# A mixture-of-experts kernel on one core: the last expert does its second half first, and second-half units are written in pairs

## The chip, the cores and the metric

The kernel runs on one core of a Trainium2 chip. The metric is the device time of one execution in microseconds, the median of three runs. Engines are named as in the profile: PE is TensorE (PEld its weight loads), DVE is VectorE, ACT is ScalarE, POOL is GpSimd, and SPq is the queue from which SyncE issues DMAs.

## The reference, cut to what matters

Three stages follow one another: a linear attention with decaying state over 4 x 8 heads, an MLP with squared ReLU (384 to 2048 to 384) over 3072 tokens, and a mixture of 8 experts, of which each token uses the two with the highest noisy logits. The change touches the last stage alone:

```python
out = np.zeros((N, D), dtype=np.float32)          # 3072 x 384
for e in range(E):                                 # 8 experts
    for k in range(2):
        mask = top2[:, k] == e
        h = np.maximum(x[mask] @ w1[e], 0.0)       # 384 -> 1024
        out[mask] += top2_w[mask, k, None] * (h @ w2[e])   # 1024 -> 384
```

## The kernel before, in words

Every product of two float32 matrices is made from three matmuls: each operand is split into a high part and a low part (ScalarE rounds the high part, VectorE or GpSimd subtracts), and high x high, high x low and low x high are summed in PSUM.

Routing writes the rows of the tokens into a table in DRAM (`sent`), sorted by expert. An expert's places in the table are seven blocks of up to 128 tokens, handled as two units (line 111): unit 0 has blocks 0 to 3, 512 tokens; unit 1 has blocks 4 to 6, of which the last counts 52, 308 tokens in all. Tokens beyond these places are left to `overflow` (line 851), which runs only where there are any. The units are worked off in the `order` of line 1024: (0,0), (1,0), (0,1), (1,1), and then each expert's unit 0 and unit 1.

One unit goes like this.

- `fetch` (line 742) issues the DMAs that bring the unit's token rows, from SP; `turn` (line 758), called for each of three slices of the model dimension, transposes a slice on VectorE into the one buffer `xt`, rounds it to `xh` on ScalarE and makes `xl` on VectorE. Both happen ahead, during an earlier unit.
- `up` (line 774) is one of eight first-layer steps f: nine matmuls (three slices d, three products each) into a PSUM bank, with the weights stationary and the tokens moving, then a relu on ScalarE (`hh`) and its low part on VectorE (`hl`). The banks rotate: steps 0, 1, 3, 4, 6, 7 take two banks in turn, steps 2 and 5 a third one.
- The second layer of a unit 0, and of the last expert's unit 1, is `down` (line 797): one call per block, 24 matmuls with the tokens stationary and 384 columns of weights moving; then `scatter` (line 812) scales the block on ScalarE and adds it to the output by an indirect DMA from GpSimd.
- The second layer of the other unit 1s is `down_t` (line 826), "turned": one call for each third d of the model dimension, 24 matmuls with the weights stationary and the 308 tokens moving, then an eviction to `yT`, on VectorE for d = 1 and on ScalarE for the others. `back` (line 842) transposes each block back in three TensorE transposes, during a later unit, and scatters it.

What the other engines do on the side of a unit comes from two lists. `fill` is handed out over the steps by their costs: turn-backs of an earlier unit, a fetch, four weight splits (`conv_next`, line 1014: ScalarE `hi`, VectorE `lo`, then the DMA for weights three pieces ahead, which reuses the freed buffer), and, in a unit 0, the turns of the same expert's unit 1. `late` is put at fixed places: `put(8.8, fn)` means after second-layer call 0 (steps 0 to 7 are first-layer ones), and the fraction of a place under 8 says after which d of that step. `TURN` (line 85) holds the places of the next unit 0's three slices: after step 7, and twice after second-layer call 0. `TURN_11` (line 84) does the same for expert 0's unit 1, with three slices and four weight splits:

```python
TURN_11 = (7.3, 7.8, 8.81, 8.82, 8.83, 9.8, 9.81)
TURN = (7.8, 8.8, 8.81)
```

The order of the instructions on each engine is the order in which the source issues them (`tc.manual_schedule()`, line 116). The main loop over units is at lines 1025 to 1089. The functions that the diff touches:

Of the kernel before, what the change touches and what calls it, by code (L numbers as in the profile page):

```python
# [8 lines left out]
F32 = mybir.dt.float32  # L9
# [8 lines left out]
P = 128  # L18
# [66 lines left out]
TURN = (7.8, 8.8, 8.81)  # L85
# [3 lines left out]
def body(ctx, tc, r, k, v, w, u, w_in, w_out, w_gate, w_noise, noise, w1, w2, out):  # L89
    nc = tc.nc  # L90
# [3 lines left out]
    E, _, F2 = w1.shape  # L94
    NT = B * S
    KD = DM // P
    NF = FF // P
    NF2 = F2 // P
# [12 lines left out]
    UNITS = ((0, 4), (4, 7))  # L111
# [53 lines left out]
    def bank(tag="att", bufs=3):  # L165
        return ps.tile([P, 512], F32, name=tag, tag=tag, bufs=bufs)
# [7 lines left out]
    L, turned = {}, {}  # L174
# [513 lines left out]
    W, RW, X, GT, HT, YT, IDX = {}, {}, {}, {}, {}, {}, {}  # L688
    pools = {}
# [11 lines left out]
    NW = 4  # L701
# [26 lines left out]
    def tokens(un):  # L728
        a0, a1 = UNITS[un]
        return sum(width(a) for a in range(a0, a1))  # L730

    def width(a):
        return SOME if a == LAST - 1 else P
# [37 lines left out]
            idx = IDX[e, un] = pl.tile([P, UNITS[un][1] - UNITS[un][0]], I32, name=f"id{un}", bufs=2)  # L771
            nc.vector.tensor_copy(idx, GT[e, un][:, 1, :])

    def up(e, un, f, between=None):
        n = tokens(un)
        if f % 3 == 2:
            ph = pools["y"].tile([P, 512], F32, name="ph2")[:, :n]
        else:
            ph = bank("ph", 2)[:, :n]
        qi, fo = divmod(f, NF2 // NW)  # L780
        wh, wl = W[e, qi]
        xh, xl = X[e, un]
        sl = slice(fo * P, (fo + 1) * P)
        m = 0
        for d in range(KD):
            for wt, xt in ((wh, xh), (wh, xl), (wl, xh)):
                nc.tensor.matmul(ph, wt[:, d, sl], xt[:, d, :n], start=(m == 0), stop=(m == 3 * KD - 1))  # L787
                m += 1
            if between:
                between(d)  # L790
        hh = pools["f2"].tile([P, BLK], F32R, name=f"hh{f}")
        hl = pools["f2"].tile([P, BLK], F32R, name=f"hl{f}")
        nc.scalar.activation(hh[:, :n], ph, AF.Relu)  # L793
        nc.vector.scalar_tensor_tensor(hl[:, :n], ph, 0.0, hh[:, :n].bitcast(F32), op0=OP.max, op1=OP.subtract)  # L794
        HT[f] = hh, hl

    def down(e, un, a):
        a0, a1 = UNITS[un]
        w_ = width(a)
        sl = slice((a - a0) * P, (a - a0) * P + w_)  # L800
        py = pools["y"].tile([P, 512], F32, name="y", bufs=2)[:w_, :DM]
        m = 0
        for f in range(NF2):
            qi, fo = divmod(f, NF2 // NW)
            wh, wl = W[e, NW + qi]
            hh, hl = HT[f]
            for ht, wt in ((hh, wh), (hl, wh), (hh, wl)):
                nc.tensor.matmul(py, ht[:, sl], wt[:, fo, :], start=(m == 0), stop=(m == 3 * NF2 - 1))  # L808
                m += 1
        scatter(e, a, py)  # L810

    def scatter(e, a, py):
        w_ = width(a)
        yt = pools["f2"].tile([P, DM], F32, name="yt", bufs=3)[:w_]
        un = unit(a)
        col = a - UNITS[un][0]
        nc.scalar.activation(yt, py, AF.Copy, scale=GT[e, un][:w_, 0, col:col + 1])  # L817
        nc.gpsimd.memset(C["gap"], 0.0)
        st = nc.gpsimd.indirect_dma_start(  # L819
            out=out, in_=yt, in_offset=None, compute_op=OP.add,  # L820
            out_offset=bass.IndirectOffsetOnAxis(ap=IDX[e, un][:w_, col:col + 1], axis=0))
        for other in adds[e]:
            tc.declare_no_dep(st.ins, other.ins, reason="a token is sent to an expert once")
        adds[e].append(st)

    def down_t(e, un, d):
        n = tokens(un)
        py = pools["y"].tile([P, 512], F32, name="y", bufs=2)[:, :n]
        m = 0
        for f in range(NF2):  # L830
            qi, fo = divmod(f, NF2 // NW)
            wh, wl = W[e, NW + qi]
            hh, hl = HT[f]
            sl = slice(d * P, (d + 1) * P)
            for wt, ht in ((wh, hh), (wh, hl), (wl, hh)):
                nc.tensor.matmul(py, wt[:, fo, sl], ht[:, :n], start=(m == 0), stop=(m == 3 * NF2 - 1))  # L836
                m += 1
        if d == 0:
            YT[e] = pools["f2"].tile([P, KD, n], F32, name="yT")
        (nc.vector.tensor_copy if d == 1 else nc.scalar.copy)(YT[e][:, d, :], py)  # L840

    def back(e, un, a):
        m = width(a)
        o = (a - UNITS[un][0]) * P
        pb = bank()
        for d in range(KD):
            nc.tensor.transpose(pb[:m, d * P:(d + 1) * P], YT[e][:, d, o:o + m], ident)
        scatter(e, a, pb[:m, :DM])
# [86 lines left out]
    def run(pieces, n):  # L935
        for p in pieces[:n]:
            p()
        del pieces[:n]
# [8 lines left out]
    for j in range(NB):  # L947
        slots = [[] for _ in range(2 * NF)]

        def put(n, fn, *args):  # L950
            k = int(n)
            slots[k].append((n - k, len(slots[k]), lambda: fn(*args)))
# [61 lines left out]
    def conv_next(eng=None):  # L1014
        conv_e(*todo.pop(0), eng)
        if len(todo) >= AHEAD:
            load_e(*todo[AHEAD - 1])

    def prepare(e, un):
        return [lambda c=c: turn(e, un, c) for c in range(KD)]  # L1020


    N0 = NF2 + UNITS[0][1]
    order = [(0, 0), (1, 0), (0, 1), (1, 1)] + [(e, un) for e in range(2, E) for un in range(2)]
    for e, un in order:
        turned = un == 1 and e < E - 1
        n_up = UNITS[un][1] - UNITS[un][0]
        fill, late = [], {}

        def put(p, *fns):  # L1030
            n, d = int(p), int(p % 1 * 4)
            late.setdefault((n, 3 if n >= NF2 else d), []).extend((p, fn) for fn in fns)

        if un == 0 and e > 1:
            fill += [lambda a=a: back(e - 1, 1, a) for a in range(*UNITS[1])]
        if (e, un) == (0, 0):
            plan = [(fn, i) for fn in (r_rest, r_row) for i in range(TPB)] + [(fn,) for fn in (r_soft1, r_soft2, r_soft3, r_top1, r_top2, r_sel, r_table, r_w1, r_rank, r_w2)]
            plan += [(r_send, *divmod(i, 2)) for i in range(2 * TPB)]
            plan = [(n, lambda fn=fn, args=args: fn(NB - 1, *args)) for n, (fn, *args) in zip(ROUTE_LAST, plan)]
            plan += [(n, lambda i=i: conv_next(nc.gpsimd if i < SPLIT_POOL else nc.vector)) for i, n in enumerate(CONV_E)]  # L1040
            plan += list(zip(TURN_10, prepare(1, 0)))
            plan += [(FETCH, lambda: fetch(0, 1)), (TOTALS, totals)]
            carry = [(n - N0, fn) for n, fn in plan if n >= N0]
            for n, fn in plan:
                if n < N0:
                    put(n, fn)
        elif (e, un) == (1, 0):
            for n, fn in carry:
                put(n, fn)
            for n in range(NW):  # L1050
                put(n + 0.8, conv_next)
            put(NW + 0.8, lambda: fetch(2, 0))
            for n, fn in zip(TURN_01, prepare(0, 1)):
                put(n, fn)
            put(TURN_01[-1], lambda: fetch(1, 1))
        elif (e, un) == (0, 1):
            for n, fn in zip(TURN_11, prepare(1, 1) + [conv_next] * NW):
                put(n, fn)
        else:
            if (e, un) == (1, 1):  # L1060
                fill += [lambda a=a: back(0, 1, a) for a in range(*UNITS[1])]
            if e + 1 < E:
                fill += [lambda: fetch(e + 1, un)] + [conv_next] * NW
            elif un == 0:
                fill += [lambda: None] * NW
            if un == 0:
                fill += prepare(e, 1)
            elif e + 1 < E:
                for n, fn in zip(TURN, prepare(e + 1, 0)):
                    put(n, fn)  # L1070
                if (e, un) == (1, 1):
                    put(TURN[-1], lambda: fetch(3, 0))
        cost = [9.0 * n_up] * NF2 + [60.0 if turned else 72.0] * n_up
        left = sum(cost[:NF2] if turned else cost)

        def do(n, d):
            for _, fn in sorted(late.get((n, d), ()), key=lambda x: x[0]):
                fn()

        for n, c in enumerate(cost):  # L1080
            if n < NF2:
                up(e, un, n, lambda d: do(n, d))
            elif turned:
                down_t(e, un, n - NF2)
            else:
                down(e, un, UNITS[un][0] + n - NF2)
            run(fill, round(len(fill) * c / max(left, c) + 0.25))
            left -= c
            do(n, 3)
    f_ctx.close()  # L1090
    ps_ctx.close()
    overflow()
# [27 lines left out]
```

## Time and profile before

| | |
|---|---|
| time, median of 3 runs | 997.45 us (996.15 to 999.99) |
| profiled execution: span from first to last instruction | 993.8 us |
| profiled execution: time of its own beside the span | not listed apart |
| TensorE busy | 959.2 us, 97% of the span |
| TensorE weight loads busy | 828.1 us, 83% |
| VectorE, ScalarE, GpSimd busy | 546.8, 437.6, 349.6 us |
| second expert layer in the chain of waits | PE y L808 14%, PE y L836 6% of the span |

The page gives the busy time of every engine, then the span in 40 slices, the DMA queues, the chain of work that ended last, and the costliest groups of instructions. The expert stage fills the second half of the span. In the timelines a line gives the start, the duration, the engine, the line of the kernel, the operation and its output and inputs; in brackets stand the idle time before it and what released it. A line's duration can be longer than the distance to the next one on its engine, as instructions overlap at their ends.

### The profile page before, as it was taken

Reading aid. Unit: us, or ns where it says so; the run is one execution under the profiler, and the core shown is the slowest. Engines: PE = TensorE matmul, PEld = TensorE weight load, DVE = VectorE, ACT = ScalarE, POOL = GpSimd, SP = SyncE. Lnnn points to the kernel's source line nnn. Section 1 sums busy time; section 2 is a strip of 40 time slices with the busy share of each in tenths; the row PEclk is TensorE's granted clock in tenths of the full one; section 3 lists DMA queues with packets and bytes.
Section 4 is the critical chain, followed back from the end, with each engine's and each line's share of the span. In section 5 each row is a group of like instructions: output and inputs, shape, how many; then the busy total and the mean of one; then the engine's idle time right before and its main releaser. Section 6 shows DMA issues by size and latency. Waiting matters only on the chain.

```text
span 993.8 us, 17485 instructions
## 1 busy us (share of the span) xinstructions
PE 959.2 (97%) x6807; PEld 828.1 (83%) x6807; DVE 546.8 (55%) x985; ACT 437.6 (44%) x795; POOL 349.6 (35%) x407
## 2 busy tenths in 40 slices
PE   7888999998999999999998999999999999999995
PEld 5666788777778878877886989989999998989895
DVE  7999956534845774572343753554445454544320
ACT  4666745333434444443653642543334334444321
POOL 5555462543563454443030352112121212212121
PEclk7999999999999999999999999999999999999998
DMA  7654469939332343231024457565454454554121
GB/s 174 154 151 144 120 157 299 246 90 278 82 108 62 68 119 78 55 78 51 16 97 110 125 139 130 128 134 117 103 108 110 101 124 91 108 110 74 20 32 22
DMA packets 193291, 112.19 MB, mean 113 GB/s; under 512 B 131728, under 2 KB 185776, under 8 KB 193200
## 3 DMA queue, kind: packets, MB, share of 16 engines
q1 hardware_dynamic: 181776, 91.22, 36.4%
q0 software_dynamic: 10624, 19.74, 10.7%
q8 instruction: 55, 0.90, 0.4%
q14 instruction: 36, 0.29, 0.1%
q10 hardware_dynamic: 800, 0.02, 0.0%
HBM read 74.83 MB, written 36.12 MB: 112 GB/s over the span
## 4 chain that ended last, share of the span: by engine, by line
PE 79%; DVE 9%; DMA 4%; SPq 2%; ACT 2%; issue 2%; POOL 1%; POOLq 0%; ACTq 0%; DVEq 0%
PE ph L787 21%; PE ph L492 15%; PE xo L515 15%; PE y L808 14%; PE y L836 6%; PE att L430 3%; PE att L412 2%; DVE t L269 2%; PE att L548 1%; DVE t L268 1%; DVE gl L504 1%; DMA stg<-in_moe_w_in 1%; DVE t L267 1%; DVE t L273 1%; SPq L535 1%
## 5 line engine op out<-in xcount | busy, mean ns | idle before, releaser
L819 POOL DMA_INDIRECT out<-yt,id x56 | 87.1, 1555 | 326.5 <-ACT yt L817 285.0
L504 DVE TENSOR_TENSOR gl<-g,gh 128x512 fp32r<-128x512 f32 x96 | 84.6, 881 | 142.0 <-ACT gh L502 138.3
L794 DVE SCALAR_TENSOR_TENSOR hl<-ph,hh 128x512 fp32r<-128x512 f32 (+1 forms) x128 | 74.6, 583 | 139.7 <-ACT hh L793 139.5
L787 PE MATMUL ph<-xh,w0h 128*128 128x308 f32 (+1 forms) x384 | 135.4, 353 | 0.0
L787 PE MATMUL ph<-xh,w0l 128*128 128x308 f32 (+1 forms) x384 | 133.5, 348 | 0.0
L787 PE MATMUL ph<-xl,w0h 128*128 128x308 f32 (+1 forms) x384 | 133.3, 347 | 0.0
L498 ACT ACTIVATE rt<-ph 128x512 f32<-128x512 f32 x96 | 57.1, 595 | 159.7 <-PE ph L492 151.2
L492 PE MATMUL ph<-x1h,wih 128*128 128x512 f32 x288 | 117.9, 409 | 1.9 <-ACT rt L498 1.3
L515 PE MATMUL xo<-gh,woh 128*128 128x512 f32 x288 | 115.1, 399 | 2.0 <-ACT gh L502 2.0
L515 PE MATMUL xo<-gh,wol 128*128 128x512 f32 x288 | 112.4, 390 | 0.9 <-POOL wol L282 0.9
L515 PE MATMUL xo<-gl,woh 128*128 128x512 f32 x288 | 112.6, 391 | 0.4 <-DVE gl L504 0.4
L492 PE MATMUL ph<-x1l,wih 128*128 128x512 f32 x288 | 112.7, 391 | 0.3 <-DVE x1l L476 0.3
L492 PE MATMUL ph<-x1h,wil 128*128 128x512 f32 x288 | 112.3, 390 | 0.0
L793 ACT ACTIVATE hh<-ph 128x512 fp32r<-128x512 f32 (+1 forms) x128 | 65.4, 512 | 100.7 <-PE ph L787 92.1
L808 PE MATMUL y<-w1h,hh 128*128 128x384 f32 (+1 forms) x280 | 93.7, 335 | 0.0
L808 PE MATMUL y<-w1l,hh 128*128 128x384 f32 (+1 forms) x280 | 93.7, 335 | 0.0
L808 PE MATMUL y<-w1h,hl 128*128 128x384 f32 (+1 forms) x280 | 93.6, 334 | 0.0
L787 PEld LDWEIGHTS ph<-xh,w0l 128*128 128x128 f32 x384 | 72.2, 188 | 8.0
L787 PEld LDWEIGHTS ph<-xl,w0h 128*128 128x128 f32 x384 | 72.3, 188 | 6.9
L787 PEld LDWEIGHTS ph<-xh,w0h 128*128 128x128 f32 x384 | 72.3, 188 | 6.7
L676 POOL DMA_INDIRECT sent<-row,si x48 | 50.1, 1043 | 70.5 <-DVE si L668 50.8
L492 PEld LDWEIGHTS ph<-x1h,wih 128*128 128x128 f32 x288 | 54.0, 187 | 18.5 <-issue 2.8
(194 smaller groups left out, 1961.4 us busy)
## 6 DMA issues: line engine op xcount, KB each, us to landing
ws<-in_moe_w SPq DMA_DIRECT2D x128, 96.0 KB
ws<-in_moe_w SPq DMA_DIRECT2D x32, 384.0 KB
sent<-zero SPq DMA_DIRECT2D x8, 1375.5 KB
G<-sent SPq DMA_DIRECT2D x36, 192.0 KB
stg<-in_moe_w_in SPq DMA_DIRECT2D x8, 768.0 KB
stg<-in_moe_w_out SPq DMA_DIRECT2D x8, 768.0 KB
out<-zero SPq DMA_DIRECT2D x1, 4800.0 KB
lv<-in_v SPq DMA_DIRECT2D x24, 192.0 KB
```

What stands on the lines that cost most here:

```text
L430: nc.tensor.matmul(pb[32 * n:32 * n + 32, d, :], x, y, skip_group_check=True, **kw)
L492: nc.tensor.matmul(ph, wt[qi][:, d, sl], xt[j][:, d, :], start=(n == 0), stop=(n == 3 * KD - 1))
L498: nc.scalar.activation(rt, ph, AF.Relu)
L504: nc.vector.tensor_tensor(gl, g, gh.bitcast(F32), op=OP.subtract)
L515: nc.tensor.matmul(XO[j][:, d, :], wt[qi][:, fo, sl], gt, start=(f == 0 and n == 0), stop=(f == NF - 1 and n == 2))
L676: st = nc.gpsimd.indirect_dma_start(out=sent, in_=s["row"][:, i, :], in_offset=None, out_offset=bass.IndirectOffsetOnAxis(ap=s["si"][:, i, ...
L787: nc.tensor.matmul(ph, wt[:, d, sl], xt[:, d, :n], start=(m == 0), stop=(m == 3 * KD - 1))
L793: nc.scalar.activation(hh[:, :n], ph, AF.Relu)
L794: nc.vector.scalar_tensor_tensor(hl[:, :n], ph, 0.0, hh[:, :n].bitcast(F32), op0=OP.max, op1=OP.subtract)
L808: nc.tensor.matmul(py, ht[:, sl], wt[:, fo, :], start=(m == 0), stop=(m == 3 * NF2 - 1))
L819: st = nc.gpsimd.indirect_dma_start(out=out, in_=yt, in_offset=None, compute_op=OP.add, out_offset=bass.IndirectOffsetOnAxis(ap=IDX[e, un] ...
L836: nc.tensor.matmul(py, wt[:, fo, sl], ht[:, :n], start=(m == 0), stop=(m == 3 * NF2 - 1))
```

## The change

The last expert does its unit 1 before its unit 0, and its unit 1 becomes turned as in the other experts; so all unit 1s are turned. Turning the last expert's unit-1 tokens is moved to the end of expert 6's unit 1, and turning its unit-0 tokens into the fill of its own unit 1. The loop over a unit 1 is written anew for all experts: first-layer steps come in pairs (`up_some`: the matmuls of both steps, then both relus, then the fill and late work of both), and the turned second layer comes as a pair of thirds 0 and 1 (the matmuls of both, both evictions, then the fill and late work of both) and third 2 alone. Unit 0s are as before.

```diff
--- before.py
+++ after.py
@@ -771,12 +771,10 @@
             idx = IDX[e, un] = pl.tile([P, UNITS[un][1] - UNITS[un][0]], I32, name=f"id{un}", bufs=2)
             nc.vector.tensor_copy(idx, GT[e, un][:, 1, :])
 
-    def up(e, un, f, between=None):
-        n = tokens(un)
-        if f % 3 == 2:
-            ph = pools["y"].tile([P, 512], F32, name="ph2")[:, :n]
-        else:
-            ph = bank("ph", 2)[:, :n]
+    def up_bank(f):
+        return pools["y"].tile([P, 512], F32, name="ph2") if f % 3 == 2 else bank("ph", 2)
+
+    def up_mm(e, un, f, ph, n, between=None):
         qi, fo = divmod(f, NF2 // NW)
         wh, wl = W[e, qi]
         xh, xl = X[e, un]
@@ -784,10 +782,26 @@
         m = 0
         for d in range(KD):
             for wt, xt in ((wh, xh), (wh, xl), (wl, xh)):
-                nc.tensor.matmul(ph, wt[:, d, sl], xt[:, d, :n], start=(m == 0), stop=(m == 3 * KD - 1))
+                nc.tensor.matmul(ph[:, :n], wt[:, d, sl], xt[:, d, :n], start=(m == 0), stop=(m == 3 * KD - 1))
                 m += 1
             if between:
                 between(d)
+
+    def up(e, un, f, between=None):
+        ph = up_bank(f)
+        up_mm(e, un, f, ph, tokens(un), between)
+        relu(un, f, ph)
+
+    def up_some(e, fs):
+        ph = [up_bank(f) for f in fs]
+        for f, p in zip(fs, ph):
+            up_mm(e, 1, f, p, tokens(1))
+        for f, p in zip(fs, ph):
+            relu(1, f, p)
+
+    def relu(un, f, ph):
+        n = tokens(un)
+        ph = ph[:, :n]
         hh = pools["f2"].tile([P, BLK], F32R, name=f"hh{f}")
         hl = pools["f2"].tile([P, BLK], F32R, name=f"hl{f}")
         nc.scalar.activation(hh[:, :n], ph, AF.Relu)
@@ -823,21 +837,23 @@
             tc.declare_no_dep(st.ins, other.ins, reason="a token is sent to an expert once")
         adds[e].append(st)
 
-    def down_t(e, un, d):
-        n = tokens(un)
-        py = pools["y"].tile([P, 512], F32, name="y", bufs=2)[:, :n]
-        m = 0
-        for f in range(NF2):
-            qi, fo = divmod(f, NF2 // NW)
-            wh, wl = W[e, NW + qi]
-            hh, hl = HT[f]
+    def down_t(e, ds):
+        py = [pools["y"].tile([P, 512], F32, name="y", bufs=2) for d in ds]
+        n = tokens(1)
+        for d, p in zip(ds, py):
+            m = 0
             sl = slice(d * P, (d + 1) * P)
-            for wt, ht in ((wh, hh), (wh, hl), (wl, hh)):
-                nc.tensor.matmul(py, wt[:, fo, sl], ht[:, :n], start=(m == 0), stop=(m == 3 * NF2 - 1))
-                m += 1
-        if d == 0:
-            YT[e] = pools["f2"].tile([P, KD, n], F32, name="yT")
-        (nc.vector.tensor_copy if d == 1 else nc.scalar.copy)(YT[e][:, d, :], py)
+            for f in range(NF2):
+                qi, fo = divmod(f, NF2 // NW)
+                wh, wl = W[e, NW + qi]
+                hh, hl = HT[f]
+                for wt, ht in ((wh, hh), (wh, hl), (wl, hh)):
+                    nc.tensor.matmul(p[:, :n], wt[:, fo, sl], ht[:, :n], start=(m == 0), stop=(m == 3 * NF2 - 1))
+                    m += 1
+        for d, p in zip(ds, py):
+            if d == 0:
+                YT[e] = pools["f2"].tile([P, KD, n], F32, name="yT")
+            (nc.vector.tensor_copy if d == 1 else nc.scalar.copy)(YT[e][:, d, :], p[:, :n])
 
     def back(e, un, a):
         m = width(a)
@@ -1021,9 +1037,9 @@
 
 
     N0 = NF2 + UNITS[0][1]
-    order = [(0, 0), (1, 0), (0, 1), (1, 1)] + [(e, un) for e in range(2, E) for un in range(2)]
+    order = [(0, 0), (1, 0), (0, 1), (1, 1)] + [(e, un) for e in range(2, E - 1) for un in range(2)]
+    order += [(E - 1, 1), (E - 1, 0)]
     for e, un in order:
-        turned = un == 1 and e < E - 1
         n_up = UNITS[un][1] - UNITS[un][0]
         fill, late = [], {}
 
@@ -1031,8 +1047,12 @@
             n, d = int(p), int(p % 1 * 4)
             late.setdefault((n, 3 if n >= NF2 else d), []).extend((p, fn) for fn in fns)
 
-        if un == 0 and e > 1:
+        if (e, un) == (1, 1):
+            fill += [lambda a=a: back(0, 1, a) for a in range(*UNITS[1])]
+        elif e > 1 and un == (e == E - 1):
             fill += [lambda a=a: back(e - 1, 1, a) for a in range(*UNITS[1])]
+        elif (e, un) == (E - 1, 0):
+            fill += [lambda a=a: back(e, 1, a) for a in range(*UNITS[1])]
         if (e, un) == (0, 0):
             plan = [(fn, i) for fn in (r_rest, r_row) for i in range(TPB)] + [(fn,) for fn in (r_soft1, r_soft2, r_soft3, r_top1, r_top2, r_sel, r_table, r_w1, r_rank, r_w2)]
             plan += [(r_send, *divmod(i, 2)) for i in range(2 * TPB)]
@@ -1057,36 +1077,51 @@
             for n, fn in zip(TURN_11, prepare(1, 1) + [conv_next] * NW):
                 put(n, fn)
         else:
-            if (e, un) == (1, 1):
-                fill += [lambda a=a: back(0, 1, a) for a in range(*UNITS[1])]
             if e + 1 < E:
                 fill += [lambda: fetch(e + 1, un)] + [conv_next] * NW
-            elif un == 0:
-                fill += [lambda: None] * NW
-            if un == 0:
-                fill += prepare(e, 1)
+            if un == (e == E - 1):
+                fill += prepare(e, 1 - un)
             elif e + 1 < E:
-                for n, fn in zip(TURN, prepare(e + 1, 0)):
+                for n, fn in zip(TURN, prepare(e + 1, int(e + 1 == E - 1))):
                     put(n, fn)
                 if (e, un) == (1, 1):
                     put(TURN[-1], lambda: fetch(3, 0))
-        cost = [9.0 * n_up] * NF2 + [60.0 if turned else 72.0] * n_up
-        left = sum(cost[:NF2] if turned else cost)
+            else:
+                fill += [lambda: None] * NW
+        cost = [9.0 * n_up] * NF2 + [60.0 if un else 72.0] * n_up
+        left = sum(cost[:NF2] if un else cost)
 
         def do(n, d):
             for _, fn in sorted(late.get((n, d), ()), key=lambda x: x[0]):
                 fn()
 
-        for n, c in enumerate(cost):
-            if n < NF2:
-                up(e, un, n, lambda d: do(n, d))
-            elif turned:
-                down_t(e, un, n - NF2)
-            else:
-                down(e, un, UNITS[un][0] + n - NF2)
-            run(fill, round(len(fill) * c / max(left, c) + 0.25))
-            left -= c
-            do(n, 3)
+        def fill_in(n):
+            c = cost[n]
+            run(fill, round(len(fill) * c / max(rest[0], c) + 0.25))
+            rest[0] -= c
+
+        rest = [left]
+        if un:
+            for n in range(0, NF2, 2):
+                up_some(e, (n, n + 1))
+                for m in (n, n + 1):
+                    for d in range(3):
+                        do(m, d)
+                    fill_in(m)
+                    do(m, 3)
+            for ds in ((0, 1), (2,)):
+                down_t(e, ds)
+                for d in ds:
+                    fill_in(NF2 + d)
+                    do(NF2 + d, 3)
+        else:
+            for n in range(len(cost)):
+                if n < NF2:
+                    up(e, un, n, lambda d: do(n, d))
+                else:
+                    down(e, un, UNITS[un][0] + n - NF2)
+                fill_in(n)
+                do(n, 3)
     f_ctx.close()
     ps_ctx.close()
     overflow()
```

## Rows read from the trace of the kernel before

**Rows 1.** Waits of TensorE's weight loads, 560 us to the end: total, times, longest.

```profile
PEld att L847 <- ACT yT L840: 0.4, 1, 0.4
```

**Rows 2.** Chain of waits, 840 us to the end: start, us, what.

```profile
862.16 10.09 PE y L836 x72
...
874.32 0.33 PE att L847 x3
...
970.90 8.36 PE y L808 x48
```

**Rows 3.** Timeline of GpSimd at the end: start, us, engine, line, operation.

```profile
980.19 1.56 POOL L819 DMA_INDIRECT out<-yt,id  x1 [2.56 <-ACT yt L817]
...
984.40 1.45 POOL L819 DMA_INDIRECT out<-yt,id  x1 [2.62 <-ACT yt L817]
```

**Rows 4.** Stretches of 0.25 us at the end; last columns: granted clock, DMA share, GB/s.

```profile
984.00:984.25 0.25, 0.00 (x0) 0.00 (x0) 0.00 (x0) 0.10 (x1) 0.00 (x0) 1.00 0.13 18
987.25:987.50 0.25, 0.00 (x0) 0.00 (x0) 0.00 (x0) 0.00 (x0) 0.00 (x0) 1.00 0.34 64
```

**Rows 5.** Timeline of VectorE in expert 4's second half.

```profile
806.76 0.96 DVE L725 TENSOR_TENSOR w1l<-ws,w1h 128x768 fp32r<-128x768 f32 x1 [0.50 <-ACT w1h L724]
...
808.36 0.48 DVE L794 SCALAR_TENSOR_TENSOR hl<-ph,hh 128x308 fp32r<-128x308 f32 x1 [0.25 <-ACT hh L793]
808.75 1.08 DVE L765 STREAM_TRANSPOSE xt<-G 128x512 f32<-128x512 f32 x1
810.53 0.69 DVE L768 TENSOR_TENSOR xl<-xt,xh 128x512 fp32r<-128x512 f32 x1 [0.70 <-ACT xh L767]
...
816.22 0.47 DVE L840 COPY yT<-y 128x308 f32<-128x308 f32 x1
```

**Rows 6.** Timeline of ScalarE in the same stretch.

```profile
807.90 0.43 ACT L793 ACTIVATE hh<-ph 128x308 fp32r<-128x308 f32 x1 [0.86 <-PE ph L787]
809.87 0.63 ACT L767 ACTIVATE xh<-xt 128x512 fp32r<-128x512 f32 x1 [1.54 <-DVE xt L765]
811.27 0.42 ACT L840 COPY yT<-y 128x308 f32<-128x308 f32 x1 [0.77 <-PE y L836]
```

**Rows 7.** Timeline of TensorE in the same stretch and after it.

```profile
810.93 0.30 PE L836 MATMUL y<-hh,w1l 128*128 128x308 f32 x1
...
817.79 0.39 PE L787 MATMUL ph<-xh,w0h 128*128 128x512 f32 x1
...
819.41 0.40 PE L787 MATMUL ph<-xl,w0h 128*128 128x512 f32 x1
```

**Rows 8.** Timeline of all engines where a matmul is held, first layer of the MLP.

```profile
74.16 0.58 ACT L498 ACTIVATE rt<-ph 128x512 f32<-128x512 f32 x1
...
74.80 0.19 PEld L492 LDWEIGHTS ph<-x1h,wih 128*128 128x128 f32 x1 [1.09 <-ACT rt L498]
...
75.14 0.40 PE L492 MATMUL ph<-x1l,wih 128*128 128x512 f32 x1
```

**Rows 9.** Timeline of all engines, expert 0's second half handing over to expert 1's.

```profile
625.76 0.42 ACT L840 COPY yT<-y 128x308 f32<-128x308 f32 x1 [0.32 <-PE y L836]
...
626.00 0.77 DVE L765 STREAM_TRANSPOSE xt<-G 128x320 f32<-128x320 f32 x1
...
632.87 0.85 ACT L724 ACTIVATE w0h<-ws 128x768 fp32r<-128x768 f32 x1 [3.40 <-DMA ws<-in_moe_w]
...
633.62 0.40 ACT L840 COPY yT<-y 128x308 f32<-128x308 f32 x1
...
634.16 0.39 PE L787 MATMUL ph<-xh,w0h 128*128 128x308 f32 x1
```

**Rows 10.** Timeline of all engines, expert 1's second half.

```profile
644.17 0.43 ACT L793 ACTIVATE hh<-ph 128x308 fp32r<-128x308 f32 x1
...
645.68 0.85 ACT L724 ACTIVATE w1h<-ws 128x768 fp32r<-128x768 f32 x1 [1.08 <-DMA ws<-in_moe_w]
...
647.44 1.08 DVE L765 STREAM_TRANSPOSE xt<-G 128x512 f32<-128x512 f32 x1
```

## The prediction

> **What bounds the kernel now.** I read the page from the top: its busy shares and its slices say that TensorE works nearly the whole span. Then came the waits, for the stretch that the change rewrites. From 560 us to the end TensorE matmuls show no wait at all and its weight loads show two, the longer one 0.4 us in total [rows 1]. So the second expert layer is bound by TensorE's own instructions, and there are two ways to move the time: fewer TensorE microseconds, or new waits. The chain of waits prices the instructions [rows 2]: a second layer with weights stationary costs 10.09 us for 72 matmuls of 308 columns (0.140 us each, so one first-layer step of nine is 1.26 us); a turn back of one block (three transposes) costs 0.33 us; a second layer with tokens stationary costs 8.36/48 = 0.174 us per matmul of 384 columns. Last, the timelines of VectorE, ScalarE and TensorE around the places where one unit hands over to the next [rows 5 to 10] show how much room the other engines have there.
>
> Besides reordering the last expert, the diff changes when ScalarE and VectorE work is written down in every second-half unit: two first-layer steps are written before their two relus, and the filling work follows the pair; the first two thirds of the turned second layer are written as a pair, and what hung on the first third (slices of the next tokens) now stands behind both evictions. TensorE's own order hardly moves. These engines take their instructions in the order written: in [rows 5] the third's eviction at 816.22 follows the last slice, just as the source has it.
>
> **What the last expert gains.** Its second half, 24 matmuls for each of three token blocks, loses 72 x 0.174 = 12.5 us and gets 10.1 us, plus three turn-backs at 3 x 0.33 = 1.0 us, all on TensorE's path: -1.4 us. Its first half is unchanged, only later, and now ends the kernel.
>
> **The tail.** The last scatter has 128 rows instead of 52. A 128-row one begins at 980.19 and its transfer ends in the slice up to 984.25; the 52-row one begins at 984.40 and ends in the slice up to 987.50 [rows 3, 4]. That is at most 4.06 against 3.10, and with slices of 0.25 us some 0.7 to 0.95 us: +0.7. Nothing follows it that could hide it.
>
> **Handing over to the next 512 tokens (experts 2 to 5).** A slice of 512 takes VectorE and ScalarE 1.08 + 0.63 + 0.69 us and three short steps between, 2.5 us in all, and the next slice waits for it, as both use one buffer [rows 5, 6]. Today slices 1 and 2 run from 811.2, under thirds 1 and 2. Now VectorE meets the eviction of third 1 first. That waits for TensorE: third 0's last matmul started at 810.93 and its eviction at 811.27, 0.34 later [rows 6, 7]; third 1 ends 3.36 us on, so the eviction starts at 814.63, and VectorE is free 0.4 us later (the next start after an operation of 0.48 us comes 0.39 after its own [rows 5]). Two slices later it is 815.02 + 5.0 = 820.0 when the low half of slice 2 exists. The next unit starts at 817.79, and its eighth matmul, due at 819.41 [rows 7], reads it. What a held matmul costs is in [rows 8]: ScalarE releases at 74.74, the weight load starts 0.06 later, the following matmul 0.40 after the release, where 0.23 is usual. So the ninth starts at 820.0 + 0.40 = 820.4 instead of 819.41 + 0.23 = 819.64: +0.76 us, four times: +3.0. The cover is third 2 and seven matmuls, 5.0 us; the work behind the eviction is now 5.7. For expert 6 the next tokens are the last expert's 320 columns; their transpose takes 0.77 us instead of 1.08 [rows 5, 9], two slices in proportion 3.6 us, until 818.6, and the eighth matmul of 308 columns is due at 817.79 + 7 x 0.14 = 818.8: 0.
>
> [...]
>
> **Experts 0 to 1.** In the unit of expert 0's second half, slice 2 and four weight splits hang on the second layer. Slice 2 started at 626.00; it must now follow third 1's eviction, due 625.76 + 3.36 = 629.12, so at 629.52: 3.52 later [rows 9]. The whole chain behind it shifts: the first split, the load that its buffer frees, the fourth split, which waits for that load to land (632.87), and behind it on ScalarE the eviction of third 2 (633.62). The first turn-back reads this eviction; it is the 0.4 us wait of [rows 1], and TensorE goes on at 634.16. With pairs the turn-back stands behind two steps instead of one, 1.26 us of grace: the added wait is 3.52 - 1.26 = +2.25 us. Bounds: 0.5 if the load lands 1.75 us sooner after its issue, 3.5 if nothing covers.
>
> **Experts 1 to 2.** That unit has three turn-backs ahead of the splits, so the first split now follows relu 5 and not relu 4. The fourth waits for its weights (645.68), and the first slice comes right behind its low half (647.44) [rows 10]: both 1.26 later, so this slice ends at 647.44 + 1.26 + 2.5 = 651.2. Third 1 ends 48 matmuls after the last step that relu at 644.17 reads, so its eviction is due at 644.17 + 6.73 = 650.9: it is 0.3 late. 0.76 + 0.3 = +1.05 us.
>
> **The last expert's own second half.** After its third pair stand slices 1 and 2 of the 512 tokens, 5.0 us on both engines, ahead of relus 6 and 7. Count from the start of the second layer: relu 3 starts 36 matmuls, one turn-back and 0.14 - 0.34 us before it, at -5.2; its low half leaves VectorE free at -5.2 + 0.46 + 0.39 = -4.3; slice 0 holds it for 2.4 more, two low halves of 0.39 each [rows 5, 6] bring it to -1.15; slices 1 and 2 end at +3.85 and low half 6, which follows, at +4.25. The twentieth matmul reads it and is due at 19 x 0.14 = +2.66. The next one starts 4.25 + 0.31 = 4.56 (0.40 less the shorter stream) instead of 2.80: +1.75 us. Bounds 1.0 to 2.3, by whether slice 0's delay counts.
>
> **Sum.** -1.4 + 0.7 + 3.0 + 2.25 + 1.05 + 1.75 = +7.35 us. The profiled execution has a span of 993.8 and would get 1001.2; the page gives no separate time for it, and the median of the runs, 997.45, lies 3.65 above its span. I carry that: 997.45 + 7.35 = **1004.8 us**. About 0.5%, 5 us, is what a measurement can tell from no change.
>
> **Rivals.**
> *It is hidden after all.* Place: VectorE between the eviction of third 1 and the next unit's eighth matmul. It decides at 0.8 us per hand-over: if two slices behind the eviction took 4.2 us and not 5.0, the third term and most of the fifth vanish, and if the same holds in the last expert and the fourth weights land early, only the shorter matmuls count: 997.45 - 1.4 + 0.7 = 996.8. For it: today's 2.5 us per slice includes waits on ScalarE behind an eviction. Against: every duration in it is a row, none depends on TensorE. 12%.
>
> *The pair waits for both banks.* Steps 6 and 7 write two PSUM banks, and step 7's is freed by low half 4. If both are waited for ahead of step 6, TensorE stops there. In experts 2 to 6 two splits now stand between low halves 3 and 4 (0.85 us on ScalarE, 0.96 on VectorE each [rows 5, 9]), and low half 4 comes to end about 8.7 us into the unit; step 7 is due at 7 x 1.26 = 8.8 and just escapes, step 6 at 7.6 would not: +1.25 in five units, 1011. Against: a wait should sit on the first writer. 10%.
>
> *The load is not the link.* The fourth split's weights come early enough to free the third's eviction: the fourth term falls to about 0.3: 1004.8 - 2.25 + 0.3 = 1002.9. For it: the landing includes issue time behind other transfers. 8%.
>
> **How the numbers follow.** The forecast gets 70%, with a range of its own of 1001.5 to 1008. The rivals get 12, 10 and 8%. The range 999.5 to 1010.5 takes in the forecast's ends, the third rival and half of the second; it leaves out most of the first. Slower by over 0.5% means above 1002.4: 0.60 of the forecast's 0.70, all of the second rival and a little of the third, 0.71; within 0.5% is 0.25, faster 0.04.
>
> **What would show it.** In the changed profile TensorE should wait for the low half of slice 2 at five hand-overs, about 0.8 us each; for the eviction of third 2 once, 2.6 us, near 635 us; and for hh and hl in the last expert's turned second layer, 1.7 us. Its last scatter should take 0.7 us more. No wait at these places and an end near 993 us of span would prove me wrong; waits at step 6 with hl as releaser would mean the second rival.

## The result and the profile after

The changed kernel takes 1004.78 us (median, 1003.34 to 1008.22) against 996.8 us for the kernel before beside it: the ratio is 1.0071, 95% interval 1.0051 to 1.0091. So it is slower, by some 7 us as the ratio has it and by 8.0 as the two medians have it. The profiled execution has a span of 1001.6 us and a time of 1003.34.

TensorE is hardly busier: the first part of the page says 961.0 us, where it was 959.2, in a span that is 7.8 us longer. It waits. The waits of its weight loads over the same stretch as [rows 1], total, times, longest:

```profile
PEld att L863 <- ACT yT L856: 2.8, 1, 2.8
PEld ph L785 <- DVE xl L768: 2.7, 5, 0.5
PEld ph L785 <- ACT xh L767: 1.7, 5, 0.4
PEld y L851 <- ACT hh L807: 0.9, 1, 0.9
PEld y L851 <- ACT yT L856: 0.8, 1, 0.8
PEld y L851 <- DVE hl L808: 0.7, 1, 0.7
PEld L649 <- issue: 0.2, 1, 0.2
```

One wait of 0.4 us has become six rows (the last one, of 0.2, is old). Lines are those of the changed kernel. The turn-back (L863) waits 2.8 us for one eviction; the first layer (L785) waits for slices at five hand-overs, each time for a high half (xh) and then for the low half (xl) of the same slice; the second layer (L851) waits for hh and hl once each, and once for an eviction.

The hand-over from expert 4 to 5 answers to [rows 5, 7]. The timeline of VectorE at the end of expert 4's second half, and then that of TensorE at the start of expert 5's first layer:

```profile
820.10 0.48 DVE L856 COPY yT<-y 128x308 f32<-128x308 f32 x1 [3.40 <-PE y L851]
820.50 1.06 DVE L765 STREAM_TRANSPOSE xt<-G 128x512 f32<-128x512 f32 x1
822.26 0.69 DVE L768 TENSOR_TENSOR xl<-xt,xh 128x512 fp32r<-128x512 f32 x1 [0.70 <-ACT xh L767]
822.99 1.07 DVE L765 STREAM_TRANSPOSE xt<-G 128x512 f32<-128x512 f32 x1
824.76 0.69 DVE L768 TENSOR_TENSOR xl<-xt,xh 128x512 fp32r<-128x512 f32 x1 [0.70 <-ACT xh L767]
```

```profile
823.26 0.39 PE L785 MATMUL ph<-xh,w0h 128*128 128x512 f32 x1
...
824.41 0.40 PE L785 MATMUL ph<-xh,w0l 128*128 128x512 f32 x1
824.78 0.50 PE L785 MATMUL ph<-xh,w0h 128*128 128x512 f32 x1
825.51 0.50 PE L785 MATMUL ph<-xl,w0h 128*128 128x512 f32 x1 [0.22 <-DVE xl L768]
825.85 0.40 PE L785 MATMUL ph<-xh,w0l 128*128 128x512 f32 x1
```

The transposes of slices 1 and 2 start at 820.50 and 822.99, behind the eviction at 820.10, which had idled VectorE for 3.40 us. In the kernel before both had run before that eviction, which starts at 816.22 [rows 5]; the second of them:

```profile
813.76 1.08 DVE L765 STREAM_TRANSPOSE xt<-G 128x512 f32<-128x512 f32 x1
```

In the changed kernel slice 2's low half ends at 825.45, the matmul that reads it starts at 825.51, and the next one 0.34 later, as in [rows 8].

The turn from expert 0 to 1 answers to [rows 9]: the transpose of slice 2 behind the eviction, the fourth split waiting for its load, and the eviction of third 2 behind it on ScalarE.

```profile
629.50 0.48 DVE L856 COPY yT<-y 128x308 f32<-128x308 f32 x1 [2.18 <-PE y L851]
...
629.90 0.76 DVE L765 STREAM_TRANSPOSE xt<-G 128x320 f32<-128x320 f32 x1
...
636.88 0.84 ACT L724 ACTIVATE w0h<-ws 128x768 fp32r<-128x768 f32 x1 [3.51 <-DMA ws<-in_moe_w]
637.63 0.40 ACT L856 COPY yT<-y 128x308 f32<-128x308 f32 x1
...
638.08 0.42 PEld L863 LDWEIGHTS att<-ident,yT 128*128 128x128 f32 x4 [2.75 <-ACT yT L856]
```

The last expert's turned second layer, where TensorE waits for what stands behind slices 1 and 2 (VectorE, then TensorE):

```profile
943.85 1.06 DVE L765 STREAM_TRANSPOSE xt<-G 128x512 f32<-128x512 f32 x1
...
946.33 1.09 DVE L765 STREAM_TRANSPOSE xt<-G 128x512 f32<-128x512 f32 x1
948.12 0.69 DVE L768 TENSOR_TENSOR xl<-xt,xh 128x512 fp32r<-128x512 f32 x1 [0.70 <-ACT xh L767]
...
948.79 0.86 DVE L808 SCALAR_TENSOR_TENSOR hl<-ph,hh 128x308 fp32r<-128x308 f32 x2
```

```profile
947.48 0.30 PE L851 MATMUL y<-hh,w1l 128*128 128x308 f32 x1
948.45 0.41 PE L851 MATMUL y<-hh,w1h 128*128 128x308 f32 x1 [0.67 <-ACT hh L807]
949.32 0.41 PE L851 MATMUL y<-hl,w1h 128*128 128x308 f32 x1 [0.47 <-DVE hl L808]
```

And the end, answering to [rows 3, 4]: the last scatter now has 128 rows.

```profile
992.08 1.56 POOL L833 DMA_INDIRECT out<-yt,id  x1 [2.56 <-ACT yt L831]
```

```profile
995.75:996.00 0.25, 0.00 (x0) 0.00 (x0) 0.00 (x0) 0.00 (x0) 0.00 (x0) 0.50 0.43 90
996.00:996.25 0.25, 0.00 (x0) 0.00 (x0) 0.00 (x0) 0.00 (x0) 0.00 (x0) 0.50 0.01 0
```

From the starts of each unit's first matmul in the timeline of TensorE, the whole difference of the spans can be laid out. Units are written (expert, unit), so (1,1) is expert 1's second half; lengths are in us.

| stretch | before | after | longer by | predicted |
|---|---|---|---|---|
| span's start to (1,1) | 632.28 | 632.66 | +0.38 | 0 |
| (1,1), first layer and turn-backs | 11.63 | 13.97 | +2.34 | +2.25 |
| (1,1) second layer to the end of (2,0)'s first | 28.05 | 29.11 | +1.06 | +1.05 |
| the same from expert 2, 3, 4, 5 to the next | 27.55, 27.69, 27.55, 27.56 | 28.29, 28.63, 28.29, 28.63 | +0.74, +0.94, +0.74, +1.07 | +0.76 each |
| expert 7, first to last matmul | 56.57 | 56.98 | +0.41 | -1.4 + 1.75 |
| last matmul to the span's end | 10.7 | 10.8 | +0.1 | +0.7 |

The sum is 7.8 us, the difference of the spans, 993.8 and 1001.6. Stretches not listed are equal to 0.02 us.

### The profile page after: what moved, and what is told of

Its sections match the earlier page's. It is cut to its first block, busy times and chain, and to the rows that moved or that the text cites. A ratio compares the mean times of both kernels' runs of the same rounds, so it can differ in the third digit from the quotient of the medians.

```text
span 1001.6 us, 17513 instructions
## 1 busy us (share of the span) xinstructions
PE 961.0 (96%) x6816; PEld 828.1 (83%) x6816; DVE 546.5 (55%) x986; ACT 436.4 (44%) x797; POOL 350.7 (35%) x407
## 4 chain that ended last, share of the span: by engine, by line
PE 75%; DVE 12%; ACT 3%; SPq 2%; DMA 2%; issue 2%; POOL 2%; POOLq 0%; ACTq 0%; DVEq 0%
PE ph L785 19%; PE ph L492 15%; PE xo L515 15%; PE y L822 13%; PE y L851 5%; PE att L430 3%; PE att L412 2%; DVE xt L765 2%; DVE t L269 2%; PE att L548 1%; DVE t L268 1%; DVE gl L504 1%; DVE t L267 1%; DVE t L273 1%; DVE xl L768 1%
## 5 line engine op out<-in xcount | busy, mean ns | idle before, releaser
L785 PE MATMUL ph<-xh,w0h 128*128 128x308 f32 (+1 forms) x384 | 136.0, 354 | 0.0
L785 PE MATMUL ph<-xl,w0h 128*128 128x308 f32 (+1 forms) x384 | 133.9, 349 | 1.1 <-DVE xl L768 1.1
L785 PE MATMUL ph<-xh,w0l 128*128 128x308 f32 (+1 forms) x384 | 133.5, 348 | 0.0
L822 PE MATMUL y<-w1h,hh 128*128 128x384 f32 x256 | 85.7, 335 | 0.0
L822 PE MATMUL y<-w1l,hh 128*128 128x384 f32 x256 | 85.6, 334 | 0.0
L822 PE MATMUL y<-w1h,hl 128*128 128x384 f32 x256 | 85.6, 334 | 0.0
L785 PEld LDWEIGHTS ph<-xl,w0h 128*128 128x128 f32 x384 | 72.3, 188 | 9.3 <-DVE xl L768 2.7
L785 PEld LDWEIGHTS ph<-xh,w0h 128*128 128x128 f32 x384 | 72.2, 188 | 8.2 <-ACT xh L767 1.7
L785 PEld LDWEIGHTS ph<-xh,w0l 128*128 128x128 f32 x384 | 72.2, 188 | 7.7
```

The lines of the kernel that those rows point to most:

```text
L785: nc.tensor.matmul(ph[:, :n], wt[:, d, sl], xt[:, d, :n], start=(m == 0), stop=(m == 3 * KD - 1))
```

## The experiments

The theory: the change is slow because VectorE and ScalarE take their work in the order written (above, the transpose at 820.50 behind the eviction at 820.10), and the pairs put slices and splits behind evictions and relus behind slices. The rivals: the paired first-layer steps or their banks cost, or the new order of the last expert does. Each kernel is the changed one with the edit shown; ratios are against the kernel before, run on the same chip. At 997 us, 0.001 in a ratio is 1 us.

**Thirds one by one.** The third loop again treats each third with its eviction and its late work; the paired steps stay.

```diff
-            for ds in ((0, 1), (2,)):
+            for ds in ((0,), (1,), (2,)):
```

> The three thirds of a turned second layer come one by one again, each with its eviction and its late work; the first-layer steps stay in pairs. Theory (slices and splits stand behind the eviction of third 1): the 0.8 us waits of TensorE for the low half of slice 2 go at experts 2 to 5 (-3.0), the wait for the eviction of third 2 near 635 us goes (-2.25 and some of the 0.4 of before), one hand-over, expert 1 to 2, keeps 0.7; the last expert's own 1.7 us stay. So about +1.8 us against the kernel before, 5.5 less than the changed kernel. Rival (the paired steps, their two banks or their late relus, are what costs): still +7 us, the waits as in the changed kernel.

Measured: 998.4 us, ratio 1.0020 (1.0006 to 1.0035), so +2.0 us where +1.8 was expected. Its waits:

```profile
PEld y L851 <- ACT hh L807: 0.9, 1, 0.9
PEld y L851 <- DVE hl L808: 0.7, 1, 0.7
PEld ph L785 <- DVE xl L768: 0.4, 1, 0.4
...
PEld att L863 <- ACT yT L856: 0.2, 1, 0.2
```

The four hand-overs are as long as before the change to 0.13 us, the wait of the turn-back is down to 0.2, one hand-over keeps 0.4, and the last expert keeps its two. No row of the list has a first-layer step waiting for its bank, so the second rival of the prediction (both banks waited for) falls; what the paired steps alone cost is told with the last three kernels below.

**Evict on the other engine.** Only the engines of two evictions are changed.

```diff
-            (nc.vector.tensor_copy if d == 1 else nc.scalar.copy)(YT[e][:, d, :], p[:, :n])
+            (nc.vector.tensor_copy if d == 2 else nc.scalar.copy)(YT[e][:, d, :], p[:, :n])
```

> Third 1 is evicted by ScalarE and third 2 by VectorE, all else as changed. Theory (VectorE's order is the link: the transposes wait behind an eviction on the same engine): the waits for slice 2 go at experts 2 to 5 (-3.0) and shrink to 0.7 at expert 1 to 2 (-0.35), the others stay: +4.0 us against the kernel before. Rival (TensorE or the banks of the paired thirds hold the hand-over, whichever engine evicts): no change, +7 us, the waits for slice 2 still there.

Measured: 1001.54 us, ratio 1.0056 (1.0034 to 1.0078). The waits for slices fell from five to one, as expected. TensorE's order and the banks are untouched by this edit, so what held the four hand-overs is the order on VectorE and ScalarE.

```profile
PEld att L863 <- DVE yT L856: 3.0, 1, 3.0
...
PEld ph L785 <- DVE xl L768: 0.5, 1, 0.5
```

The slices did not get clear of the eviction of third 1, though. It now stands on ScalarE, ahead of the rounding of slice 1 (expert 4, VectorE and then ScalarE):

```profile
814.52 1.08 DVE L765 STREAM_TRANSPOSE xt<-G 128x512 f32<-128x512 f32 x1
...
817.89 0.42 ACT L856 COPY yT<-y 128x308 f32<-128x308 f32 x1 [2.94 <-PE y L851]
818.20 0.63 ACT L767 ACTIVATE xh<-xt 128x512 fp32r<-128x512 f32 x1
```

Only the transpose of slice 1, 1.08 us, runs ahead of the eviction, and that is enough where 0.8 us were missing: slice 2's low half ends at 822.06, and the matmul that reads it starts at 822.67, unheld.

The time came out at +5.6 instead of +4.0; the interval, +3.4 to +7.8, holds both. In the profile the unit (1,1) accounts for the excess: its first layer took 15.50 us, 1.5 more than in the changed kernel, though the turn-back waited hardly longer (3.0 against 2.8). What came on top is in the granted clock, by stretches around the wait (a row has the stretch, its length, the busy us and in brackets the instructions of TensorE, its weight loads, VectorE, ScalarE and GpSimd, then clock, DMA share and GB/s):

```profile
635.00:636.00 1.00, 0.00 (x0) 0.00 (x0) 0.97 (x2) 0.63 (x3) 0.00 (x0) 0.92 0.72 267
...
637.00:638.00 1.00, 1.00 (x6) 1.00 (x5) 0.15 (x1) 0.94 (x2) 0.19 (x1) 0.50 0.76 195
638.00:639.00 1.00, 1.00 (x6) 1.00 (x5) 0.00 (x0) 0.17 (x1) 1.00 (x2) 0.50 0.97 312
...
639.50:640.50 1.00, 1.00 (x10) 1.00 (x9) 0.29 (x1) 0.43 (x1) 0.83 (x1) 1.00 0.91 219
```

While TensorE stood idle the granted clock fell to 0.50 and stayed there for some 3 us; in its timeline matmuls of 308 columns came 0.26 us apart there, and 0.14 us apart in the last row's stretch. (The counts in the rows take in instructions that reach over the edge of a stretch.) The changed kernel's own profile has the same gap, 0.2 us shorter, and no fall: its clock is 1.00 throughout this stretch.

**The first split ahead of the second layer.** In expert 0's second half, the place of one split moves.

```diff
-TURN_11 = (7.3, 7.8, 8.81, 8.82, 8.83, 9.8, 9.81)
+TURN_11 = (7.3, 7.8, 8.81, 7.9, 8.83, 9.8, 9.81)
```

> In expert 0's second half the first of the four weight splits is put before the second layer, all else as changed. Theory (the fourth split waits for the load that the first one's buffer frees, and the eviction of third 2 waits behind it on ScalarE): the load goes out some 4 us sooner, the one wait of 2.5 us or more of a turn-back goes, -2.3 to -2.6 us: +4.8 us against the kernel before. Rival (the wait comes from the evictions themselves or from another load): the wait stays, +7 us.

Measured: 1001.11 us, ratio 1.0042 (1.0027 to 1.0056): +4.2 where +4.8 was expected. The wait of the turn-back is gone from the list, the waits for slices are unchanged:

```profile
PEld ph L785 <- DVE xl L768: 2.7, 5, 0.5
PEld ph L785 <- ACT xh L767: 1.7, 5, 0.4
```

So the chain from the first split's buffer over the load to the eviction is the cause of this wait, and its length is what the first split's place sets.

**Thirds one by one and the last turns late.** As the first experiment, and the last expert's 512 tokens are turned where the other experts do it.

```diff
-                fill += prepare(e, 1 - un)
+                if un:
+                    for n, fn in zip(TURN, prepare(e, 0)):
+                        put(n, fn)
+                else:
+                    fill += prepare(e, 1)
```

> As e1_thirds_single, and the 512 tokens' slices of the last expert are turned at the places where the other experts turn theirs (after step 7 and after third 0) and no longer between the pairs. Theory (relus 6 and 7 stand behind slices 1 and 2): the last expert's waits for hh and hl, 1.7 us, go as well: about 0 against the kernel before, 1.75 less than e1_thirds_single. Rival (these waits come from the paired steps): the same time as e1_thirds_single.

Measured: 996.57 us, ratio 1.0002 (0.9989 to 1.0015), 1.8 less than the first experiment. The second layer of (7,1) takes 10.09 us, where the first experiment has 11.84. Both waits for hh and hl are gone; one wait for an eviction, at expert 1, is longer here:

```profile
PEld y L851 <- ACT yT L856: 1.3, 1, 1.3
PEld ph L785 <- DVE xl L768: 0.5, 1, 0.5
```

**Steps one by one.** The paired thirds stay, and the first-layer steps are as before the change.

```diff
-            for n in range(0, NF2, 2):
-                up_some(e, (n, n + 1))
-                for m in (n, n + 1):
-                    for d in range(3):
-                        do(m, d)
-                    fill_in(m)
-                    do(m, 3)
+            for n in range(NF2):
+                up(e, 1, n, lambda d: do(n, d))
+                fill_in(n)
+                do(n, 3)
```

> The first-layer steps come one by one again, each with its relu and its late work, as before; the paired thirds 0 and 1 stay. Theory (the paired thirds cost, the paired steps do not): the waits for slice 2 stay at all five hand-overs (+3.0 and +0.8), the wait of the turn-back for the eviction of third 2 grows to 3.5, since only one step covers it, the last expert's own wait for hh and hl stays at 1.8: about +8.5 us against the kernel before, 1 more than the changed kernel. Rival (the pairs of steps cost): +2 us or less.

Measured: 1007.89 us, ratio 1.0094 (1.0072 to 1.0117), +9.4 where +8.5 was expected. Pairing the steps had helped at one place: it put one more step ahead of the turn-back. Without it the wait is 3.9 us,

```profile
PEld att L863 <- ACT yT L856: 3.9, 1, 3.9
PEld ph L785 <- DVE xl L768: 2.7, 5, 0.5
```

and as with the 3.0 us wait above the clock fell: it was granted at 0.50 from about 640 to 643 us, which is part of the +9.4. The interval reaches down to +7.2, so that this kernel is slower than the changed one is shown by the profiles alone (1.5 us more from (1,1)'s first matmul to the last of all); the rival's +2 us or less is ruled out by the times.

**The order alone, with the last turns late, and with the split first.** Three kernels with steps and thirds one by one: only the order and the last expert's second layer are new in the first; the second adds the late turns of the fourth experiment; the third adds the edit of `TURN_11` too.

> Steps and thirds come one by one as before, so only the order and the second layer of the last expert are changed. Theory: no wait at the other experts' hand-overs; the shorter second layer gives 1.4, the longer last scatter takes 0.1 to 0.7, and slices 1 and 2 ahead of the last relus cost 1.7 to 1.9 in the last expert: +0.4 to +1.2 us against the kernel before. Rival (the new order itself is what costs): +5 us or more.

> As e6_order_alone, with the last expert's 512 tokens turned at the places of the other experts. Theory: no new wait is left; the shorter second layer less the tail, -0.7 to -1.3 us against the kernel before, hard to tell from none. Rival (something else in the new order costs): slower than the kernel before.

> As e7_order_turns_late, and the first of expert 0's four late splits is put before the second layer, so that the 0.4 us wait of the kernel before goes too: -1.1 to -1.7 us against the kernel before, 0.4 less than e7_order_turns_late. Rival (the wait of 0.4 us is hidden by other work): the same as e7_order_turns_late.

Measured: 998.69 us, ratio 1.0001 (0.9986 to 1.0016); 997.73 us, 0.9992 (0.9979 to 1.0006); 995.56 us, 0.9968 (0.9957 to 0.9980). The new order of the last expert does not cost anything by itself. In the first of the three its gain is eaten by the waits for hh and hl (0.9 and 0.7 us again); without them the kernel is level with the one before or a little faster, as far as this can be told. In the profiles of the second and third the last expert takes 55.29 us from its first to its last matmul, 1.28 less than in the kernel before, where the prediction had 1.4. The third beats both kernels: it is 3.2 us faster than the one before (2.0 to 4.3), more than the 1.1 to 1.7 that were expected. Its one row in the list of waits from 560 us on is

```profile
PEld L649 <- issue: 0.2, 1, 0.2
```

The last of the three is 2.2 us below the second in the median, where 0.4 was expected. The profiles account for half of it: from the start of (1,1) to the end of (2,0)'s first layer the third takes 1.13 us less than the second, 0.68 of it in the first layer of (1,1), where the second waits 0.7 us for the turn-back, and 0.46 in the spacing described at the end. The rest stays open.

The first of these kernels and the first experiment differ by the paired steps alone. By the ratios the pairs cost 1.9 us, with overlapping intervals; in the profiles the two take the same time from (1,1)'s first matmul to the last one of all, 351.3 us with pairs and 351.5 without. So a cost of the paired steps is not shown.

## Why the prediction was right

**The direction and the sum.** 1004.8 was forecast and 1004.78 measured. That hits closer than its parts: the forecast was made from a median of 997.45, while the kernel before had 996.8 with one more run, 0.38 us of the profiled difference came about ahead of the first changed instruction, and the 3.65 us that were carried from the span to the median came out as 3.15 in the changed kernel. That it fits to 0.02 us is luck.

**Hand-overs, experts 2 to 5.** The step was that slices 1 and 2 stand behind the eviction of third 1 and are 0.8 us too long for the cover. The eviction started 3.16 us ahead of the next unit's first matmul in both (814.63 worked out, 820.10 seen), and the loss in two of the four is 0.74 us against 0.76. The other two lost 0.94 and 1.07, for a reason that was not in the working (below). Evicting on ScalarE, which let one transpose run ahead, removed all of it but that. At these four and at the hand-over from expert 1 to 2 the matmul after the held one started 0.33 to 0.34 us behind it, as in [rows 8].

**Experts 0 to 1.** +2.34 against +2.25. Both links are shown: the split's place by the third experiment, and the one step of grace that the pairs give by the fifth, where the wait grew by 1.1 us for a forecast of 1.26.

**Experts 1 to 2.** +1.06 against +1.05, but by another way. I had slice 0 delay the eviction of third 1 by 0.3 us and with it the hand-over. The late slice 0 has one more consequence, which I left out: it also delays the eviction of third 0 on ScalarE, and third 2 waits for its bank, 0.8 us in the list of waits (L851 for yT). ScalarE, TensorE, VectorE:

```profile
653.61 0.40 ACT L856 COPY yT<-y 128x308 f32<-128x308 f32 x1
654.06 0.41 PE L851 MATMUL y<-hh,w1h 128*128 128x308 f32 x1 [0.54 <-ACT yT L856]
654.35 0.47 DVE L856 COPY yT<-y 128x308 f32<-128x308 f32 x1
```

Third 1's last matmul starts at 653.22, so its eviction was due at 653.56 and is 0.8 us late, not 0.3: the fourth split, which waits for its weights, starts 3.58 us into the second layer (650.21) where it had been 1.77 (645.68), so 1.8 us later and not 1.26. But third 2 is as late, and the first layer of (2,0) is longer by 0.71 us, hardly less than at the other hand-overs. The unit pays 0.8 for the bank and 0.7 for the slices. That the sum agrees is luck: the kernel before had lost 0.46 us in this unit to the slower spacing described below.

**The last expert.** Own waits +1.78 (11.87 us of second layer against 10.09) as against +1.75, and gone when the slices moved (fourth experiment). With the shorter second layer the expert comes out 0.41 longer, 0.35 was forecast.

**The tail.** This term was mis-sized. The transfer behaves as said, 992.08 to the stretch up to 996.00, 3.9 us instead of 3.1; but from the landing to the end of the span 5.6 us pass, and 6.3 passed before, so that the end is only 0.1 us later. Why the rest was shorter stays open; in the eight experiments, whose last scatter has 128 rows too, the time from the last matmul to the end is 10.6 to 11.0 us.

**The rivals.** That all is hidden: no, the list of waits shows them all. That pairs wait for both banks: no, no step of the changed kernel waits for a low half to free its bank, and of the 2.0 us that paired steps without paired thirds cost, 1.8 went with the last expert's turns (fourth experiment). That the load is not the link: no, moving the split removed the wait.

## What to carry to other kernels

Where the bound engine has no gaps, a reordering of the source costs by what it puts behind a wait on the other engines: write down each engine's queue around a hand-over and ask which instruction now stands behind an eviction (here two transposes, 0.74 to 1.07 us per hand-over). Evictions belong after the work that the next unit's first matmuls need; an eviction on another engine that also has a part of this work, as ScalarE has here, gains only what then runs ahead of it (one transpose of 1.08 us). Relus that the second layer reads belong ahead of the next unit's preparation (waits of 0.9 and 0.7 us in the last expert). And a load that is released by a buffer should have its releaser as early as it can be (a wait of 2.8 us went with one split).

## What was not expected of the hardware

**The clock after a wait.** In two experiments TensorE waited 3.0 and 3.9 us for the turn-back, and its clock was granted at 0.50 for some 3 us, from 0.6 us before it went on in the first and from 1.4 us after it in the second. That added some 1.3 us to the wait of 3.0 (15.50 us of first layer against 13.97, less the 0.2 that the wait was longer). In the changed kernel's profile a wait of 2.8 us at the same place left it at 1.00. So two of the three gaps had a fall and one had none; what decides that is not shown. Whether some of the timed runs of the changed kernel had such a fall is not shown. The longest of them, 1008.22 us, has the lowest mean granted clock, 0.985, where the profiled one has 0.990.

**A second spacing.** Turned second layers of 72 matmuls take 10.09 us or 10.55 us, in the changed kernel by turns (experts 2 to 5, stretches of the second layer; columns as in the rows on the clock above):

```profile
702.61:712.70 10.09, 10.09 (x74) 10.09 (x73) 4.76 (x8) 2.11 (x4) 0.00 (x0) 1.00 0.31 86
757.67:768.22 10.55, 10.55 (x74) 10.55 (x73) 5.02 (x8) 2.11 (x4) 0.00 (x0) 1.00 0.31 92
813.17:823.26 10.09, 10.09 (x74) 10.09 (x73) 4.76 (x8) 2.11 (x4) 0.00 (x0) 1.00 0.31 87
868.22:878.77 10.55, 10.55 (x74) 10.55 (x73) 4.94 (x8) 2.11 (x4) 0.00 (x0) 1.00 0.32 91
```

The clock is 1.00 in all four, TensorE waits for nothing, and DMA is alike. Only odd-numbered experts were seen slow, and not in every kernel: the kernel before has it at expert 1 alone. At experts 3 and 5 it came only in kernels with paired steps: in four of five profiles at one or both, in none of the five with single steps, the kernel before among them. So the pairs may cost up to 0.9 us in this way, which no experiment separates. The cause is open. After a slow layer the hand-over itself waits 0.1 to 0.3 us less (0.94 - 0.46 and 1.07 - 0.46 against 0.74), since a slow third 2 gives the slices 0.15 us more.
